# A fused retention and swish-MLP kernel whose every engine issues in an order written out by hand

## The chip, the cores and the metric

The kernel runs on one core of a Trainium2 chip. The metric is the device time of one execution in microseconds (us), as the median of several runs; the profile is of one further execution. The engines are named as the profile names them: PE (matrix multiply; PEld is its weight loads), DVE (vector), ACT (scalar, activations), POOL (GpSimd) and SP (the queue that issues most DMAs).

## What is computed

Eight batches of eight heads, 576 positions, head width 64. Retention without softmax, then a two-layer MLP with a swish whose slope is learned for each hidden unit. The MLP's rows are the 4608 positions, its columns the heads side by side (512).

```python
scores = scale * np.matmul(q, k.transpose(0, 1, 3, 2))
Dmat = np.where(rel >= 0, gamma[:, None, None] ** rel[None, :, :], 0.0)
x = np.matmul(scores * Dmat[None, :, :, :], v)   # then heads side by side: [4608, 512]
h = x @ w_in                                      # 512 -> 2048
g = h * (1.0 / (1.0 + np.exp(-beta * h)))
out = g @ w_out                                   # 2048 -> 512
```

## The kernel before

The decay is split into a factor on q (gq, which also holds the scale) and one on v (gv), so a batch of 576 rows is walked in five chunks: four of 128 rows and a short one of 64. A state carries what earlier chunks add. `attn_chunk(b, c)` does one chunk in these steps:

- prepare (L154 to L160): qn = q times gq, kn = k cast to bf16, vpad = v times gv, spread so that each head pair has its own columns. In batch 0 qn is made on DVE and kn on ACT, later all three on POOL.
- T (L165): eight PE transposes; ACT copies the result out of PSUM (qkT, L169, 1.0 us).
- sc (L177): eight 64-row score matmuls; DVE applies the causal mask (R, L181, twice).
- O (L189, L194): four matmuls with the state (sbd) and eight with vpad; DVE casts the sum into xT (L199), the MLP's input.
- st (L208): four matmuls that add to the state; ACT copies it twice into sbd (L215). The short chunk has none.

The MLP works in nine blocks of 512 rows. `moe_up(m)` has 16 groups of four 512-column matmuls (ph, L229), each followed by a Silu on ACT (gT, L231); `moe_down(m)` has four outputs of 16 matmuls each (po, L239), copied by DVE (ot, L242) and stored through SP (L243). All ph and po tiles share three PSUM buffers; T, O and st have one buffer each, sc two.

The weights come in four 1 MB pieces each, w_in (L126) and w_out (L132), through three staging buffers; DVE casts each w_in piece in one instruction (L127) and scales each w_out piece in four (L135). Chunks are loaded as three DMAs of 256 KB (q, k, v, L60) into seven staging buffers.

The order of each engine's instructions is chosen by the framework's scheduler from priorities that follow the program text: batch 0, then for each later batch its loads, its five chunks, and the up and down of the block before. Only within a chunk's sc, O and st matmuls is PE's order fixed by hand. Loads of w_out stand behind the chunks of batch 1 on SP.

Of the kernel before, what the change touches and what calls it, by code (L numbers as in the profile page):

```python
# [11 lines left out]
F32 = mybir.dt.float32  # L12
# [7 lines left out]
def kernel(  # L20
# [15 lines left out]
    P = 128  # L36
# [26 lines left out]
    for c in range(NC):  # L63
        load_chunk(0, c)
# [3 lines left out]

    ident_f = consts.tile([P, P], F32, name="ident_f")
# [20 lines left out]

    NV = 3
    vpads = []
    for i in range(NV):
        vp = consts.tile([P, H, P], BF16, name=f"vpad{i}")
        nc.gpsimd.memset(vp[:], 0.0)
        vpads.append(vp)

    NS = 2
    sbds = []
    for i in range(NS):  # L100
        s = consts.tile([P, HP, P], BF16, name=f"sbd{i}")
        nc.gpsimd.memset(s[:], 0.0)
        sbds.append(s)
# [19 lines left out]
    w_out_r = moe_w_out.rearrange("(fo fi) n -> fi fo n", fi=P)  # L123
    for g in range(WG):
        t = stage.tile([P, KO, FG], F32, name="wt", tag="wt", bufs=3)
        nc.sync.dma_start(t[:], w_in_r[:, :, g * FG:(g + 1) * FG])  # L126
        nc.vector.tensor_copy(w_in_sb[:, :, g * FG:(g + 1) * FG], t[:])  # L127

    def load_w_out():
        for g in range(WG):  # L130
            t = stage.tile([P, KO, d_model], F32, name="wt", tag="wt", bufs=3)
            nc.sync.dma_start(t[:], w_out_r[:, g * KO:(g + 1) * KO, :])  # L132
            for i in range(KO):
                fo = g * KO + i
                nc.vector.tensor_scalar(w_out_sb[:, fo, :], t[:, i], rbeta_sb[:, fo:fo + 1], None, ALU.mult)  # L135
# [4 lines left out]
    cnt = [0]  # L140

    def attn_chunk(b, c):
        c0, cL = chunks[c]
        t = qkv_tiles.pop((b, c))
        first = b == 0
        qn = sb.tile([P, H, D], BF16, name="qn", tag="qn", bufs=2)
        kn = sb.tile([P, H, D], BF16, name="kn", tag="kn", bufs=3)
        vp = vpads[cnt[0] % NV]
# [4 lines left out]
        eq = nc.vector if first else nc.gpsimd  # L153
        eq.tensor_tensor(qn[:cL], t[:cL, 0], gq_b, ALU.mult)  # L154
# [4 lines left out]
        nc.gpsimd.tensor_tensor(vp4[:cL], t[:cL, 2].rearrange("p (pr two) d -> p pr two d", two=2),  # L159
                                gv_b.rearrange("p (pr two) d -> p pr two d", two=2), ALU.mult)  # L160

        T = psum.tile([P, 2, HP, P], BF16, name="T", tag="T", bufs=1)
        for i, src in enumerate((qn, kn)):
            for p in range(HP):
                nc.tensor.transpose(T[:, i, p, :cL],  # L165
                                    src[:cL, 2 * p:2 * p + 2, :].rearrange("p h d -> p (h d)"),
                                    ident[:cL, :cL])
        qkT = sb.tile([P, 2, HP, P], BF16, name="qkT", tag="qkT", bufs=3)
        nc.scalar.copy(qkT[:, :, :, :cL], T[:, :, :, :cL])  # L169

        R = sb.tile([P, 2, HP, P], BF16, name="R", tag="R", bufs=2)
        sc = [psum.tile([P, HP, P], F32, name="sc", tag="sc", bufs=2) for _ in range(2)]
        with tc.manual_schedule(engines={PE}):
            for p in range(HP):
                for j in range(2):
                    r = slice(j * D, (j + 1) * D)
                    nc.tensor.matmul(sc[j][:cL, p, :cL], qkT[r, 1, p, :cL], qkT[r, 0, p, :cL],  # L177
                                     start=True, stop=True, skip_group_check=True)
# [5 lines left out]
        with tc.manual_schedule(engines={PE}):  # L184
            n = 0
            if c > 0:
                sbd = sbds[(cnt[0] - 1) % NS]
                for p in range(HP):
                    nc.tensor.matmul(O[:, p, :cL], sbd[:, p, :], qkT[:, 0, p, :cL],  # L189
                                     start=(n == 0), stop=False, skip_group_check=True)  # L190
                    n += 1
            for p in range(HP):
                for j in range(2):
                    nc.tensor.matmul(O[:, p, :cL], vp[:cL, 2 * p + j, :], R[:cL, j, p, :cL],  # L194
                                     start=(n == 0), stop=(p == HP - 1 and j == 1),
                                     skip_group_check=True)
                    n += 1
        n0 = b * S + c0
        nc.vector.tensor_copy(xT[:, :, n0:n0 + cL], O[:, :, :cL])  # L199

        if c < NC - 1:
            if c == 0:
                st = psum.tile([P, HP, P], F32, name="st", tag="st", bufs=1)
                state_ps[b] = st
            st = state_ps[b]
            with tc.manual_schedule(engines={PE}):
                for p in range(HP):
                    nc.tensor.matmul(st[:, p, :],  # L208
                                     kn[:cL, 2 * p:2 * p + 2, :].rearrange("p h d -> p (h d)"),
                                     vp4[:cL, p], start=(c == 0 and p == 0), stop=True,  # L210
                                     skip_group_check=True)
            sbd = sbds[cnt[0] % NS]
            for j in range(2):
                r = slice(j * D, (j + 1) * D)
                nc.scalar.copy(sbd[r, :, j * D:(j + 1) * D], st[r, :, j * D:(j + 1) * D])  # L215
        cnt[0] += 1
# [4 lines left out]
    def moe_up(m, fos):  # L221
        m0 = m * MB
# [3 lines left out]
        for fo in fos:  # L226
            ph = psum.tile([P, MB], F32, name="ph", tag="mm", bufs=3)
            for ko in range(KO):
                nc.tensor.matmul(ph[:], w_in_sb[:, ko, fo * P:(fo + 1) * P], xT[:, ko, m0:m0 + MB],  # L229
                                 start=(ko == 0), stop=(ko == KO - 1))  # L230
            nc.scalar.activation(gT[:, fo, :], ph[:], ACT.Silu, scale=beta_sb[:, fo:fo + 1])  # L231

    def moe_down(m):
        m0 = m * MB
        gT = gts.pop(m)
        for ms in range(MB // P):
            po = psum.tile([P, d_model], F32, name="po", tag="mm", bufs=3)
            for fo in range(FO):
                nc.tensor.matmul(po[:], gT[:, fo, ms * P:(ms + 1) * P], w_out_sb[:, fo, :],  # L239
                                 start=(fo == 0), stop=(fo == FO - 1))  # L240
            ot = sb.tile([P, d_model], F32, name="ot", tag="ot", bufs=3)
            nc.vector.tensor_copy(ot[:], po[:])  # L242
            nc.sync.dma_start(out[m0 + ms * P:m0 + (ms + 1) * P, :], ot[:])  # L243

    for c in range(NC):
        attn_chunk(0, c)
    for b in range(1, B + 1):
        if b < B:
            for c in range(NC):
                load_chunk(b, c)  # L250
                if b == 1 and c == NC - 1:
                    load_w_out()
            for c in range(NC):
                attn_chunk(b, c)
        moe_up(b - 1, range(FO))
        moe_down(b - 1)
    for m in range(B, NMB):
        moe_up(m, range(FO))
        moe_down(m)
# [30 lines left out]
```

## Time and profile before

| | us |
|---|---|
| median of 3 runs | 362.81 |
| range of the runs | 362.46 to 363.98 |
| the profiled execution, its time | 362.31 |
| its span, first to last instruction | 360.6 |
| PE busy in the span | 335.3 |
| ACT busy | 160.7 |
| DVE busy | 112.5 |
| POOL busy | 102.6 |

Work on the row of PE includes the time in which a matmul drains while the next already runs, so its busy time is no measure of how densely matmuls follow each other; the distances between starts are. The mean granted TensorE clock over the span is 0.962 of full speed.

### The profile page before, as it was taken

Reading aid. Unit: us, or ns where it says so; the run is one execution under the profiler, and the core shown is the slowest. Engines: PE = TensorE matmul, PEld = TensorE weight load, DVE = VectorE, ACT = ScalarE, POOL = GpSimd, SP = SyncE. Lnnn points to the kernel's source line nnn. Section 1 sums busy time; section 2 is a strip of 40 time slices with the busy share of each in tenths; the row PEclk is TensorE's granted clock in tenths of the full one; section 3 lists DMA queues with packets and bytes.
Section 4 is the critical chain, followed back from the end, with each engine's and each line's share of the span. In section 5 each row is a group of like instructions: output and inputs, shape, how many; then the busy total and the mean of one; then the engine's idle time right before and its main releaser. Section 6 shows DMA issues by size and latency. Waiting matters only on the chain.

```text
span 360.6 us, 5795 instructions
## 1 busy us (share of the span) xinstructions
PE 335.3 (93%) x2369; PEld 175.9 (49%) x2369; DVE 112.5 (31%) x196; ACT 160.7 (45%) x257; POOL 102.6 (28%) x124
## 2 busy tenths in 40 slices
PE   1768967999999999999999999999999999999995
PEld 1643455345544644465446544654466444444442
DVE  4565144724422630164025402450146011011011
ACT  2653843017720864076506660567047703703810
POOL 6211760026832761085007600670051000000000
PEclk9976975799999999999999999999999999999999
DMA  9998995769938995599569951300110011011002
GB/s 175 211 351 209 219 235 208 191 163 219 203 73 200 179 202 92 157 241 192 114 166 206 215 100 58 106 0 2 58 60 2 0 58 60 0 58 59 2 34 82
DMA packets 121978, 46.52 MB, mean 129 GB/s; under 512 B 113232, under 2 KB 113248, under 8 KB 121952
## 3 DMA queue, kind: packets, MB, share of 16 engines
q1 hardware_dynamic: 121920, 46.15, 56.2%
q8 instruction: 18, 0.29, 0.4%
q14 instruction: 8, 0.07, 0.1%
q10 hardware_dynamic: 32, 0.01, 0.0%
HBM read 36.71 MB, written 9.44 MB: 128 GB/s over the span
## 4 chain that ended last, share of the span: by engine, by line
PE 88%; ACT 5%; DVE 3%; DMA 1%; SPq 1%; issue 1%; POOL 0%; ACTq 0%
PE po L239 35%; PE ph L229 34%; PE O L194 6%; PE T L165 5%; PE sc L177 4%; ACT qkT L169 4%; PE O L189 2%; PE st L208 2%; DVE R L181 1%; DMA qkvn<-in_k_dram 1%; SPq L60 1%; ACT gT L231 0%; DVE w_in_sb L127 0%; POOL qn L154 0%; DVE xT L199 0%
## 5 line engine op out<-in xcount | busy, mean ns | idle before, releaser
L229 PE MATMUL ph<-xT,w_in_sb 128*128 128x512 bf16 x576 | 140.2, 384 | 1.7 <-DVE w_in_sb L127 1.7
L231 ACT ACTIVATE gT<-ph,beta_sb 128x512 bf16<-128x512 f32 x144 | 98.9, 687 | 67.4 <-PE ph L229 66.7
L239 PE MATMUL po<-w_out_sb,gT 128*128 128x512 bf16 x576 | 127.5, 383 | 0.9 <-DVE w_out_sb L135 0.9
L239 PEld LDWEIGHTS <-gT 128*128 128x128 bf16 x576 | 56.8, 99 | 69.9 <-issue 3.1
L169 ACT COPY qkT<-T 128x1024 bf16<-128x1024 bf16 (+1 forms) x40 | 36.9, 924 | 100.0 <-PE T L165 100.0
L229 PEld LDWEIGHTS <-w_in_sb 128*128 128x128 bf16 x576 | 53.0, 99 | 56.2 <-issue 3.1
L242 DVE COPY ot<-po 128x512 f32<-128x512 f32 x36 | 24.7, 691 | 168.6 <-PE po L239 168.6
L154 POOL TENSOR_TENSOR qn<-qkvn,gq 128x512 bf16<-128x512 f32 (+1 forms) x35 | 36.6, 1046 | 127.6 <-issue 45.1
L181 DVE TENSOR_TENSOR R<-sc,causal 128x512 bf16<-128x512 f32 (+1 forms) x80 | 47.0, 628 | 35.0 <-PE sc L177 35.0
L159 POOL TENSOR_TENSOR vpad<-qkvn,gv 128x512 bf16<-128x512 f32 (+1 forms) x40 | 41.8, 1045 | 30.4 <-DMA qkvn<-in_v_dram 23.6
L199 DVE CAST xT<-O 128x512 bf16<-128x512 f32 (+1 forms) x40 | 25.5, 638 | 31.9 <-PE O L194 31.8
L194 PE MATMUL O<-R,vpad 128*128 128x128 bf16 (+1 forms) x320 | 31.7, 226 | 2.4 <-DVE R L181 2.2
L194 PEld LDWEIGHTS <-vpad 128*128 128x128 bf16 (+1 forms) x320 | 23.1, 103 | 13.9 <-issue 6.8
L215 ACT CAST sbd<-st 64x256 bf16<-64x256 f32 x64 | 23.4, 366 | 8.8 <-PE st L208 8.0
L177 PE MATMUL sc<-qkT 64*128 64x128 bf16 (+1 forms) x320 | 17.3, 226 | 9.5 <-ACT qkT L169 8.8
L158 POOL CAST kn<-qkvn 128x512 bf16<-128x512 f32 (+1 forms) x35 | 21.3, 607 | 11.0 <-DMA qkvn<-in_k_dram 10.6
L177 PEld LDWEIGHTS <-qkT 64*128 64x128 bf16 (+1 forms) x320 | 10.0, 102 | 20.5 <-ACT qkT L169 18.2
L165 PE MATMUL T<-ident,qn 128*128 128x128 bf16 (+1 forms) x160 | 16.1, 226 | 3.4 <-DVE qn L154 3.3
L165 PE MATMUL T<-ident,kn 128*128 128x128 bf16 (+1 forms) x160 | 17.7, 227 | 0.0
L165 PEld LDWEIGHTS <-qn 128*128 128x128 bf16 (+1 forms) x160 | 10.4, 102 | 9.2 <-DVE qn L154 3.6
L208 PE MATMUL st<-vpad,kn 128*128 128x128 bf16 x128 | 13.6, 230 | 0.0
L189 PE MATMUL O<-qkT,sbd 128*128 128x128 bf16 (+1 forms) x128 | 12.4, 223 | 0.1
(32 smaller groups left out, 59.7 us busy)
## 6 DMA issues: line engine op xcount, KB each, us to landing
out_dram<-ot SPq DMA_DIRECT2D x36, 256.0 KB, 2.0
qkvn<-in_q_dram SPq DMA_DIRECT2D x32, 256.0 KB, 4.9
qkvn<-in_k_dram SPq DMA_DIRECT2D x32, 256.0 KB, 5.1
qkvn<-in_v_dram SPq DMA_DIRECT2D x32, 256.0 KB, 5.1
wt<-in_moe_w_in_dram SPq DMA_DIRECT2D x4, 1024.0 KB, 8.3
wt<-in_moe_w_out_dram SPq DMA_DIRECT2D x4, 1024.0 KB, 7.2
qkvn<-in_q_dram SPq DMA_DIRECT2D x8, 128.0 KB, 4.5
qkvn<-in_k_dram SPq DMA_DIRECT2D x8, 128.0 KB, 4.2
```

What stands on the lines that cost most here:

```text
L154: eq.tensor_tensor(qn[:cL], t[:cL, 0], gq_b, ALU.mult)
L159: nc.gpsimd.tensor_tensor(vp4[:cL], t[:cL, 2].rearrange("p (pr two) d -> p pr two d", two=2), gv_b.rearrange("p (pr two) d -> p pr two d", ...
L165: nc.tensor.transpose(T[:, i, p, :cL], src[:cL, 2 * p:2 * p + 2, :].rearrange("p h d -> p (h d)"), ident[:cL, :cL])
L169: nc.scalar.copy(qkT[:, :, :, :cL], T[:, :, :, :cL])
L177: nc.tensor.matmul(sc[j][:cL, p, :cL], qkT[r, 1, p, :cL], qkT[r, 0, p, :cL], start=True, stop=True, skip_group_check=True)
L181: nc.vector.tensor_tensor(R[:cL, j, :, :cL], sc[j][:cL, :, :cL], m_b, ALU.mult)
L194: nc.tensor.matmul(O[:, p, :cL], vp[:cL, 2 * p + j, :], R[:cL, j, p, :cL], start=(n == 0), stop=(p == HP - 1 and j == 1), skip_group_check ...
L199: nc.vector.tensor_copy(xT[:, :, n0:n0 + cL], O[:, :, :cL])
L229: nc.tensor.matmul(ph[:], w_in_sb[:, ko, fo * P:(fo + 1) * P], xT[:, ko, m0:m0 + MB], start=(ko == 0), stop=(ko == KO - 1))
L231: nc.scalar.activation(gT[:, fo, :], ph[:], ACT.Silu, scale=beta_sb[:, fo:fo + 1])
L239: nc.tensor.matmul(po[:], gT[:, fo, ms * P:(ms + 1) * P], w_out_sb[:, fo, :], start=(fo == 0), stop=(fo == FO - 1))
L242: nc.vector.tensor_copy(ot[:], po[:])
```

## The change

All engines now run under a manual schedule: every instruction stands on its engine in the order in which the program text issues it. The text is rewritten for that.

- `attn_chunk` is split into steps: `pre` (qn, kn, vpad), `a_T`, `a_sc`, `a_st`, `a_O`. The MLP is split into groups: `up(m, fo)` with four matmuls, `down(m, ms, f0)` with four. `merged` walks a list of groups and puts the attention steps between them at given group numbers: `attn_steps` puts `pre` four groups ahead of a_T, a_sc two groups behind a_T, and a_st and a_O two groups behind a_sc.
- Only chunks 0 to 3 run ahead of the MLP, with `pre` two chunks ahead and 22 extra 512-column matmuls on a zero tile in all (`warm_up`): 12 at the start and 2 at five places. Then the 16 up groups of block 0 follow, with chunks 4 and 5 between the last of them.
- Block 1's up is done in two parts: its first 192 columns (chunks 4 and 5) before block 0's down, its other 320 after it. Chunks 6, 7 and 8 stand between these.
- From block 2 on, the chunks that block m+1 needs (4 or 5) are spread evenly over block m's 32 groups.
- SP loads four chunks, w_in, three chunks, w_out, and then one chunk for each that has been prepared. The staging buffers of weights grow from three to four and also hold the outputs (`ot`, four to a tile). Of each weight piece three quarters are cast on DVE and one on POOL.
- Three small things: gq's scale moves into the exponent as a bias; the second half of O walks one half of R after the other; two memsets move to DVE.

SP, the loads of w_out; each qkvn tile is a chunk, each wt tile a piece of 1 MB. Before:

```order
L60 DMA qkvn_450<-in_q_dram 64x8x64
L60 DMA qkvn_450<-in_k_dram 64x8x64
L60 DMA qkvn_450<-in_v_dram 64x8x64
L132 DMA wt_454<-in_moe_w_out_dram 128x4x512
L132 DMA wt_460<-in_moe_w_out_dram 128x4x512
L132 DMA wt_466<-in_moe_w_out_dram 128x4x512
L132 DMA wt_472<-in_moe_w_out_dram 128x4x512
```

The changed kernel:

```order
L63 DMA qkvn_152<-in_q_dram 128x8x64
L63 DMA qkvn_152<-in_k_dram 128x8x64
L63 DMA qkvn_152<-in_v_dram 128x8x64
L133 DMA wt_435<-in_moe_w_out_dram 128x4x512
L133 DMA wt_437<-in_moe_w_out_dram 128x4x512
L133 DMA wt_467<-in_moe_w_out_dram 128x4x512
L133 DMA wt_469<-in_moe_w_out_dram 128x4x512
```

Before, w_out stands behind ten chunks (qkvn_450 is the short one of batch 1); now behind seven (qkvn_152 is chunk 6).

DVE at the end of the first chunks, where the MLP begins. Before:

```order
L199 CAST xT<-O 128x4x128
L181 TENSOR_TENSOR R<-sc,causal 64x4x64 x2
L199 CAST xT<-O 128x4x64
L127 CAST w_in_sb<-wt 128x4x512 x4
L181 TENSOR_TENSOR R<-sc,causal 128x512 x2
```

The changed kernel:

```order
L221 TENSOR_TENSOR R<-sc,causal 128x512 x2
L129 CAST w_in_sb<-wt 128x512 x3
L242 CAST xT<-O 128x4x128
L129 CAST w_in_sb<-wt 128x512 x9
L221 TENSOR_TENSOR R<-sc,causal 64x4x64 x2
```

The first weights are now cast between R and xT of chunk 3, where before all five chunks went first; the short chunk's R follows the weights.

ACT in the middle of the kernel: Silu (gT), copies of T (qkT) and of the state (sbd). Before, a batch from its third full chunk on:

```order
L169 COPY qkT<-T 128x1024
L215 CAST sbd_129<-st 64x4x64 x2
L231 ACTIVATE gT<-ph,beta_sb 128x512
L169 COPY qkT<-T 128x1024
L215 CAST sbd_127<-st 64x4x64 x2
L231 ACTIVATE gT<-ph,beta_sb 128x512
L169 COPY qkT<-T 128x8x64
L231 ACTIVATE gT<-ph,beta_sb 128x512 x13
```

The changed kernel, block 2's up:

```order
L275 ACTIVATE gT<-ph,beta_sb 128x512 x4
L261 CAST sbd_126<-st 64x4x64 x2
L275 ACTIVATE gT<-ph,beta_sb 128x512 x3
L205 COPY qkT<-T 128x8x64
L275 ACTIVATE gT<-ph,beta_sb 128x512 x6
L205 COPY qkT<-T 128x1024
L275 ACTIVATE gT<-ph,beta_sb 128x512 x3
```

Before, a batch's copies stand close together with a Silu between two chunks and then 13 Silus in a row; now three to six Silus stand between one copy and the next.

The diff, cut; the steps a_T, a_sc, a_st and a_O hold the instructions of `attn_chunk`, unchanged but for the order inside O.

```diff
+    ctx.enter_context(tc.manual_schedule())
...
+    NQ = 7
+    order = [(b, c) for b in range(B) for c in range(NC)]
+    for b, c in order[:4]:
+        load_chunk(b, c)
...
+    nc.scalar.activation(gq[:], lg[:], ACT.Exp, bias=lscale[:])
...
+    def cast_w_in(g):
+        t = wts.pop(g)
+        for ko in range(KO):
+            e = nc.gpsimd if ko == KO - 1 else nc.vector
+            e.tensor_copy(w_in_sb[:, ko, g * FG:(g + 1) * FG], t[:, ko])
...
+    for b, c in order[4:NQ]:
+        load_chunk(b, c)
+
+    def warm_up(n):
+        ph = psum.tile([P, MB], F32, name="ph", tag="mm", bufs=3)
+        for _ in range(n):
+            nc.tensor.matmul(ph[:], warm[:, :P], warm[:], start=True, stop=True, skip_group_check=True)
...
+        for j in range(2):
+            for p in range(HP):
+                nc.tensor.matmul(O[:, p, :cL], vp[:cL, 2 * p + j, :], R[:cL, j, p, :cL],
+                                 start=(n == 0), stop=(j == 1), skip_group_check=True)
...
+    def up(m, fo, t0=0, tn=MB):
...
+    def down(m, ms, f0, fn=4):
...
+            if ms == 0:
+                ots[m] = stage.tile([P, MB // P, d_model], F32, name="ot", tag="wt", bufs=4)
...
+    def merged(fill, *streams):
+
+        todo = sorted((x for st in streams for x in st), key=lambda x: x[0])
+        for n, f in enumerate(fill):
+            while todo and todo[0][0] <= n:
+                todo.pop(0)[1]()
+            f()
+        for _, step in todo:
+            step()
...
+    def attn_steps(i, at, gap=2.0):
+
+        return [(at - 4, F(pre, i)), (at - 3.9, F(load_next, i)), (at, F(a_T, i)), (at + gap, F(a_sc, i)),
+                (at + 2 * gap, F(a_st, i)), (at + 2 * gap, F(a_O, i))]
+
+    warm_up(12)
+    betas()
+    pre(0)
+    a_T(0)
+    nc.gpsimd.memset(vpads[2][:], 0.0)
+    pre(1)
+    for i in range(4):
+        warm_up(2)
+        a_sc(i)
+        a_st(i)
+        if i < 3:
+            a_T(i + 1)
+            if i < 2:
+                pre(i + 2)
+        else:
+            cast_w_in(0)
+            warm_up(2)
+        a_O(i)
+
+    fill = [F(up, 0, fo) for fo in range(FO)]
+    merged(fill, [(2, F(cast_w_in, 1)), (5, F(cast_w_in, 2)), (9, F(cast_w_in, 3))],
+           [(5.1 + g / 10, F(load_w_out, g)) for g in range(2)],
+           [(9.1 + g / 10, F(load_w_out, g)) for g in range(2, WG)],
+           [(9.5, F(pre, 4)), (12, F(a_T, 4)), (14, F(a_sc, 4)), (16, F(a_O, 4))],
+           [(9.6, F(pre, 5)), (15, F(a_T, 5)), (16.1, F(a_sc, 5))], [(9.7, F(pre, 6))])
+    for i in range(5):
+        load_next(i)
+
+    q1 = S + chunks[0][1] - MB
+    a_st(5)
+    a_O(5)
...
+    fill = [F(up, 1, fo, 0, q1) for fo in range(FO)]
+    fill += [F(down, 0, ms, f0) for f0 in range(0, FO, 4) for ms in range(3)]
+    fill += [F(down, 0, 3, f0) for f0 in range(0, FO, 4)]
+    n1 = len(fill)
+    fill += [F(up, 1, fo, q1, MB - q1) for fo in range(FO)]
+    fill += [F(down, 1, ms, f0) for ms in range(MB // P) for f0 in range(0, FO, 4)]
+    streams = [[(4, F(cast_w_out, 0)), (10, F(cast_w_out, 1)), (18, F(cast_w_out, 2)), (21, F(cast_w_out, 3))],
+               [(0, F(a_T, 6)), (4, F(a_sc, 6)), (8, F(a_st, 6)), (8, F(a_O, 6))],
+               attn_steps(7, 23), attn_steps(8, 27)]
...
+    for m in range(2, NMB):
+        base = len(fill)
+        fill += [F(up, m, fo) for fo in range(FO)]
+        fill += [F(down, m, ms, f0) for ms in range(MB // P) for f0 in range(0, FO, 4)]
+        if m + 1 < NMB:
+            todo = list(range(done, need(m + 1)))
+            streams += [attn_steps(i, base + n * 31 / len(todo)) for n, i in enumerate(todo)]
+            done = need(m + 1)
+    merged(fill, *streams)
```

## Rows read from the trace of the kernel before

**Rows 1.** Chain that ended last, in order of time: start us, us, what.

```profile
63.66 15.68 PE po L239 x64
...
79.33 0.45 PE T L165 x8
...
139.73 13.81 PE po L239 x64
...
153.54 0.46 PE T L165 x8
...
190.53 0.46 PE T L165 x8
...
342.96 13.83 PE po L239 x64
...
356.81 0.69 DVE ot L242
```

**Rows 2.** Stretches: busy us of each engine, granted TensorE clock, DMA share, GB/s.

```profile
23.00:33.00 10.00, 7.38 (x46) 3.58 (x45) 5.70 (x8) 3.71 (x5) 0.00 (x0) 0.50 0.77 272
...
51.00:66.00 15.00, 10.86 (x94) 7.38 (x93) 8.61 (x18) 4.07 (x7) 1.86 (x3) 0.50 0.56 198
```

**Rows 3.** Timeline of the first 30 us: start us, us, engine, line, what, waits.

```profile
17.61 1.04 POOL L159 TENSOR_TENSOR vpad<-qkvn,gv 128x512 bf16<-128x512 f32 x1 [2.74 <-DMA qkvn<-in_v_dram]
...
17.75 0.76 ACT L215 CAST sbd<-st 64x256 bf16<-64x256 f32 x2 [0.88 <-PE st L208]
...
21.46 1.29 DVE L181 TENSOR_TENSOR R<-sc,causal 128x512 bf16<-128x512 f32 x2 [1.48 <-PE sc L177]
...
23.75 0.69 DVE L199 CAST xT<-O 128x512 bf16<-128x512 f32 x1 [0.40 <-PE O L194]
...
27.08 3.60 DVE L127 CAST w_in_sb<-wt 128x2048 bf16<-128x2048 f32 x3
...
28.36 1.89 PE L229 MATMUL ph<-xT,w_in_sb 128*128 128x512 bf16 x4 [1.65 <-DVE w_in_sb L127]
```

**Rows 4.** Stretches of 1 us, loading chunks, then weights (columns as above).

```profile
12.00:13.00 1.00, 1.00 (x11) 0.79 (x10) 1.00 (x2) 0.94 (x3) 0.00 (x0) 1.00 1.38 217
...
24.00:25.00 1.00, 0.33 (x9) 0.17 (x8) 0.44 (x1) 0.70 (x2) 0.00 (x0) 0.50 1.05 387
```

**Rows 5.** Timeline where batch 4 meets the first half of block 3.

```profile
153.38 0.39 PE L165 MATMUL T<-ident,qn 128*128 128x128 bf16 x4
...
153.82 0.39 PE L208 MATMUL st<-vpad,kn 128*128 128x128 bf16 x4
...
154.05 1.03 PE L229 MATMUL ph<-xT,w_in_sb 128*128 128x512 bf16 x4
...
154.08 1.01 ACT L169 COPY qkT<-T 128x1024 bf16<-128x1024 bf16 x1 [13.63 <-PE T L165]
...
155.15 0.40 PE L177 MATMUL sc<-qkT 64*128 64x128 bf16 x8
...
155.48 0.40 PE L165 MATMUL T<-ident,qn 128*128 128x128 bf16 x4
```

**Rows 6.** The same chain: pieces of a full and a short chunk.

```profile
122.72 0.39 PE O L194 x7
...
126.07 0.23 PE T L165 x8
...
128.69 0.24 PE sc L177 x7
...
129.68 0.12 PE O L189 x4
...
130.68 0.31 PE O L194 x7
```

**Rows 7.** Costliest groups of the page: two kinds of work on ACT.

```profile
L231 ACT ACTIVATE gT<-ph,beta_sb 128x512 bf16<-128x512 f32 x144 | 98.9, 687 | 67.4 <-PE ph L229 66.7
...
L215 ACT CAST sbd<-st 64x256 bf16<-64x256 f32 x64 | 23.4, 366 | 8.8 <-PE st L208 8.0
```

More of the change, by code (lines that the diff above doesn't have):

```diff
@@ L123 @@
     w_out_r = moe_w_out.rearrange("(fo fi) n -> fi fo n", fi=P)
-    for g in range(WG):
[L125 to L135, printed above, removed]
+    wts = {}
@@ L152, in attn_chunk @@
         gv_b = gv[:cL, c, :].unsqueeze(2).to_broadcast([cL, H, D])
[L153 to L154 removed]
+        (nc.vector if first else nc.gpsimd).tensor_tensor(qn[:cL], t[:cL, 0], gq_b, ALU.mult)
         if first:
@@ L169, in attn_chunk, with a_sc @@
         nc.scalar.copy(qkT[:, :, :, :cL], T[:, :, :, :cL])
+        L["qT"], L["kT"] = qkT[:, 0], qkT[:, 1]
+    def a_sc(i):
+        b, c = order[i]
+        c0, cL = chunks[c]
+        L = live[i]
         R = sb.tile([P, 2, HP, P], BF16, name="R", tag="R", bufs=2)
         sc = [psum.tile([P, HP, P], F32, name="sc", tag="sc", bufs=2) for _ in range(2)]
[L173 to L178, printed above, removed]
+        for p in range(HP):
+            for j in range(2):
+                r = slice(j * D, (j + 1) * D)
+                nc.tensor.matmul(sc[j][:cL, p, :cL], L["kT"][r, p, :cL], L["qT"][r, p, :cL],
+                                 start=True, stop=True, skip_group_check=True)
         m_b = causal[:cL, :cL].unsqueeze(1).to_broadcast([cL, HP, cL])
@@ L181, in attn_chunk @@
             nc.vector.tensor_tensor(R[:cL, j, :, :cL], sc[j][:cL, :, :cL], m_b, ALU.mult)
-        O = psum.tile([P, HP, P], F32, name="O", tag="O", bufs=1)
[L184 to L191, printed above, removed]
-            for p in range(HP):
[L193 to L197, printed above, removed]
+        L["R"] = R
@@ L198, in attn_chunk @@
         n0 = b * S + c0
         nc.vector.tensor_copy(xT[:, :, n0:n0 + cL], O[:, :, :cL])
[L201 to L215, printed above, removed]
@@ L216, in attn_chunk, with a_st @@
-        cnt[0] += 1
+        del live[i]
+    def a_st(i):
+        b, c = order[i]
+        c0, cL = chunks[c]
+        L = live[i]
+        if c == NC - 1:
+            return
+        if c == 0:
+            state_ps[b] = psum.tile([P, HP, P], F32, name="st", tag="st", bufs=1)
+        st = state_ps[b]
+        for p in range(HP):
+            nc.tensor.matmul(st[:, p, :], L["kn"][:cL, 2 * p:2 * p + 2, :].rearrange("p h d -> p (h d)"),
+                             L["vp4"][:cL, p], start=(c == 0 and p == 0), stop=True,
+                             skip_group_check=True)
+        sbd = sbds[i % NS]
+        for j in range(2):
+            r = slice(j * D, (j + 1) * D)
+            nc.scalar.copy(sbd[r, :, j * D:(j + 1) * D], st[r, :, j * D:(j + 1) * D])
@@ L225, in moe_up @@
         gT = gts[m]
[L226 to L259, printed above, removed]
+        x0 = m * MB + t0
+        ph = psum.tile([P, MB], F32, name="ph", tag="mm", bufs=3)
@@ new lines @@
+    done = 9
+    need = lambda m: min(len(order), next((i + 1 for i, (b, c) in enumerate(order)
+                                          if b * S + chunks[c][0] + chunks[c][1] >= (m + 1) * MB), len(order)))
+    todo = list(range(done, need(2)))
+    streams += [attn_steps(i, n1 + n * 30 / len(todo)) for n, i in enumerate(todo)]
+    done = need(2)
+    for m in range(2, NMB):
[6 more added lines that the diff above has]
+            done = need(m + 1)
```

133 lines of the change are left out of this document (93 added, 40 removed).

## The prediction

> **What bounds the kernel now.** I read the chain of work in order of time first: it lies on PE nearly throughout, so the question is how much of PE's time is work that has to be done. In the chain 64 matmuls of 512 columns take 13.81 us when nothing disturbs them, 0.863 us for a group of four [rows 1]. The MLP is 18 such halves, 18 x 13.81 = 248.6 us. An attention chunk is priced from starts in a dense stretch [rows 5]: eight T from 153.38 to 153.82, 0.44; four st to 154.05, 0.23; eight sc from 155.15 to 155.48, 0.33; eight O with vpad at 0.39 for seven, 0.45 [rows 6]; four O with the state as half the T, 0.22. That is 1.67 for a full chunk, 1.45 for the first of a batch (no state to read). The short one is 0.23 + 8/7 x 0.24 + 0.12 + 8/7 x 0.31 = 0.98 [rows 6]. A batch is 1.45 + 3 x 1.67 + 0.98 = 7.44, eight are 59.5. So 308 us of the 360.6 are dense PE work.
>
> Where the other 52 lie shows in the chain [rows 1]. Block 0's down begins at 63.66, with 13.81 + 2 x 7.44 = 28.7 of work done: 35.0 lost. From there to the end of the last po, 342.96 + 13.83 = 356.79, there are 293.1 us for 17 x 13.81 + 6 x 7.44 = 279.4: 13.7 lost. A batch in the middle, from 153.54 to 190.53, takes 36.99 for 27.62 + 7.44, so 1.9 are lost in each. One such loss can be seen: T begins at 153.38, ACT copies it from 154.08 for 1.01, sc begins at 155.15, and four ph fill only part of the gap [rows 5]. The last 3.8 us are copy and store of the last output. [...]
>
> **The start.** Before, all of batch 0 comes ahead of the first ph at 28.36, and all of batch 1 ahead of the first po. Now only four chunks come first. Their twelve DMAs are the first twelve on SP in both kernels, so the last v lands at 17.61 as before, where POOL waited for it [rows 3], and its k one DMA (262 KB at 217 GB/s [rows 4] = 1.2 us) earlier, at 16.4. From there the chain on hand-ordered engines is: kn cast 0.7 (taken as long as xT's), four T 0.22, the two sbd copies queued on ACT 0.76, qkT 1.01, sc 0.33, R 1.29, three w_in casts on DVE of a quarter of 1.2 each, 0.9, and xT 0.69 [rows 3, 5]; with about nine hand-overs of 0.06 (154.08 + 1.01 to 155.15 [rows 5]) that is 6.4, or 22.8. The first MB of w_in follows chunk 3 at 387 GB/s [rows 4], 2.7 us, and is there at 20.3, in time. A half clock doubles sc and T in this gappy stretch, so I take **23.5** for the first ph (22.5 to 26). The 22 warm-up matmuls cost 22 x 0.22 to 0.43 of PE time, but stand where PE waits for landings, qkT or R; uncovered, the last two pairs would cost 1.7, which is in the 26.
>
> The first ph will run at half clock, I think: the warm-ups are too few to make these chunks dense. Before, the first down after such a stretch took 15.68 instead of 13.81 [rows 1], and the first four ph 1.89 with their drain [rows 3]. I take **2.0** lost, from 0 to 2.3.
>
> **Weights and chunks in time.** From 20.3 three more MB of w_in land by 28.4, chunks 4 to 6 (2.5 x 786 KB at 217) by 37.5, w_out by 48.3. Up groups 4, 8 and 12 want the later pieces at 27, 30.5 and 34 or after; chunk 4's T stands at group 12, some 10 us behind the first ph, and its loads are done at 30.2. The first down comes at about 51.5, its last quarter of w_out is wanted nine groups later. Chunk 7 lands at 51.9 and is wanted at 57.5. POOL, with 2.7 us of preparation for a chunk and a fourth of each cast, sits on none of these. Stores and loads share SP, so a load queues behind a store that waits for ot, but each load is seven chunks ahead of its use. All of this I cost at nothing; if SP came later than I think by 5 us, PE would wait those 5.
>
> **Where PE must wait in the hand order.** (a) Between chunks 4 to 6: T of chunk 5 has one up group and O of chunk 4 (0.86 + 0.4) before its sc, but ACT has a Silu and then the copy to do; then O of chunk 5 has only st in front, while R takes 1.29. Walking ACT, DVE and PE with these durations I get 0.3 + 1.1 = 1.4. (b) In the first part of block 1's up a group of 192 columns takes PE about 0.33 and its Silu about 0.4 (estimate between the 0.366 of a 256-column copy and the 0.687 of a 512-column Silu [rows 7]); with qkT and sbd on ACT in the same 16 groups PE ends 1.4 late. (c) The 320-column part: 0.3. Together **3.1**.
>
> (d) The steady part. T is followed by two groups, so sc comes 0.44 + 2 x 0.863 = 2.17 after T's start. With an idle ACT it could come 1.77 after it [rows 5]. If the Silu of the group before is still running, ACT is free 0.94 instead of 0.70 after T's start, which makes 2.01: still 0.16 to spare. O comes 1.73 + 0.45 behind sc, R needs 1.29. So most of the 1.9 per batch goes away; I leave 0.05 per chunk, **1.5** (0 to 9.5, see the first rival).
>
> **The sum.** 23.5 + 248.6 + seven batches and a short chunk, 7 x 7.44 + 0.98 = 53.1, + 2.0 + 3.1 + 1.5 = 331.8 for the end of the last po; + 3.8 = 335.6 of span; the profiled execution took 362.31 for a span of 360.6, so + 1.7 = 337.3; the median is 0.5 above it: **337.8**. The gain of 25.0 is some 14 at the start (at 63.66 the changed kernel has done 28.7 + 14 of work) and 11 in the steady part.
>
> [...]
>
> **Rivals.** First: ACT runs one Silu late in the up groups. Then sc waits 0.69 - 0.16 = 0.53 at each of the 18 or so chunks whose T stands there: 9.5 more, **347** (342 to 352). For it: 16 Silus are 11.0 us and 2.6 chunks of copies 4.6, 15.6 of the 18 us of an up phase. Against it: three PSUM buffers let PE run ahead, and downs have no Silu. Chance 0.17.
>
> Second: the MLP starts late. The clock is at half through the first chunks, every step between landing and landing is longer, first ph at 26.5: **341**, and 345 with w_out pushed back as well. For it: the clock of before [rows 2]. Chance 0.10.
>
> Third, slower: ACT becomes the bound. Its strict order lets a Silu that waits for PE hold the copy that PE waits for; with two Silus and not one ahead, each of 36 chunks pays 2 x 0.69 - 0.16 = 1.2, 43 in all: **381**. It is slower than before from 0.7 per chunk on. Against it: PE's order puts the group's matmuls ahead of each such Silu. Chance 0.05.
>
> [...] Chance 0.01.
>
> Fifth: no half clock at the first ph, no waits but (a): **331**. Chance 0.04.
>
> **How the numbers follow.** Forecast 0.61 (332 to 342), first rival 0.17, second 0.10, slower 0.06, faster than 332 0.04, and 0.02 that waits eat just the gain. The range goes from 331 to 347: it leaves out the slower cases, the equal one and the upper half of the first rival, about 0.17. About 0.5% is what a measurement here can tell from no change. Faster 0.92, same 0.02, slower 0.06.
>
> **What would show it.** First ph near 23.5; first po near 51 instead of 63.66; no half clock after about 28; between two down halves of the middle blocks 27.6 plus 6 to 8 us instead of 37; sc's wait for qkT nearly gone from the waits. Wrong would be: a chain with qkT or R in every chunk, DVE or POOL waiting for w_out or chunk 7, or a second stretch at half clock.

## The result and the profile after

The changed kernel takes 338.43 us (median of 4 runs, 338.11 to 338.8); the kernel before, run beside it, 362.63. The ratio is 0.934, with a 95% interval of 0.929 to 0.939. The profiled execution took 338.8 for a span of 337.1, at a mean granted clock of 0.994.

The chain in order of time (start us, us, what) answers [rows 1]: the way to the first po, the first po of block 1, the T at the ends of two blocks in the middle, the last po. A T that stands at the same place in two blocks bounds one whole block.

```profile
35.56 7.35 DMA wt<-in_moe_w_out_dram
...
46.28 2.66 PE ph L273 x32
48.94 6.04 PE po L285 x28
...
78.69 0.86 PE po L285 x4
...
131.47 0.45 PE T L201 x8
...
165.55 0.45 PE T L201 x8
...
201.41 0.45 PE T L201 x8
...
319.47 13.83 PE po L285 x64
```

Block 0's down begins at 48.94 and not at 63.66. By then PE has done 13.81 of up, 10.56 of chunks (batch 0 and chunks 5 and 6) and 5.18 of block 1's up (192 of 512 columns), 29.55 in all, so 19.4 are lost up to there, where 35.0 were lost before: 15.6 gained. The last po ends at 319.47 + 13.83 = 333.30. From 48.94 that is 284.36 for 278.55 of dense work (17 x 13.81 - 5.18 of MLP, and 48.96 for 26 full and 7 short chunks), so 5.8 are lost where 13.7 were: 7.9 gained. Together that is the 23.5 by which the last po ends earlier.

The stretches (busy us of PE, PEld, DVE, ACT and POOL with counts, granted clock, DMA share, GB/s) answer [rows 2]:

```profile
8.00:12.00 4.00, 3.36 (x29) 2.26 (x30) 1.75 (x4) 1.87 (x3) 1.72 (x2) 0.57 1.37 218
23.00:33.00 10.00, 9.82 (x47) 4.25 (x46) 4.53 (x9) 7.72 (x12) 3.97 (x5) 1.00 1.06 256
...
51.00:66.00 15.00, 14.97 (x118) 8.08 (x117) 6.80 (x12) 3.49 (x6) 11.72 (x14) 1.00 1.24 204
```

Both stretches that were at 0.50 are at 1.00. PE is busy for 14.97 of the 15 us from 51 to 66, where it was for 10.86. The half clock is left only among the first chunks, 0.57 from 8 to 12.

The timeline of the start answers [rows 3]:

```profile
22.28 9.01 PE L273 MATMUL ph<-xT,w_in_sb 128*128 128x512 bf16 x41 [1.34 <-DVE xT L242]
```

The first ph comes at 22.28 (28.36 before) behind xT, and 41 of them follow in 9.01 us, 0.22 each, at a granted clock of 1.00 from 22 to 24 and from 23 to 33. Before, the first four took 1.89, their drain included [rows 3].

The waits (who, for whom: us of idle time, times, us of the longest) show where the steady gain is:

```profile
PE sc L217 <- ACT qkT L205: 0.4, 2, 0.2
```

The same two waits of the kernel before:

```profile
PE sc L177 <- ACT qkT L169: 8.8, 8, 2.4
```

sc hardly waits for ACT's copy any more (0.4 for 8.8, and the 0.4 lies in the first 30 us). And a chunk in the middle of the changed kernel, which answers [rows 5]:

```profile
156.70 0.39 PE L201 MATMUL T<-ident,qn 128*128 128x128 bf16 x4
...
157.15 1.89 PE L285 MATMUL po<-w_out_sb,gT 128*128 128x512 bf16 x8
...
157.35 1.01 ACT L205 COPY qkT<-T 128x1024 bf16<-128x1024 bf16 x1 [3.54 <-PE T L201]
...
158.97 0.23 PEld L217 LDWEIGHTS <-qkT 64*128 64x128 bf16 x8 [0.42 <-issue]
158.97 0.40 PE L217 MATMUL sc<-qkT 64*128 64x128 bf16 x8
159.30 1.90 PE L285 MATMUL po<-w_out_sb,gT 128*128 128x512 bf16 x8
...
161.04 0.39 PE L255 MATMUL st<-vpad,kn 128*128 128x128 bf16 x4
```

The copy ends at 158.36, while the two groups of po still run (157.15 + 8 x 0.2158 = 158.88). sc begins 2.27 us behind T's start. From 159.30 to st at 161.04 there are 8 x 0.2158 and nothing else. The one gap left is that of 0.09 to 0.10 between the last po and sc; it comes back below.

### The profile page after: what moved, and what is told of

It reads as the page before. It is cut to its first block, busy times and chain, and to the rows that moved or that the text cites. A ratio compares the mean times of both kernels' runs of the same rounds, so it can differ in the third digit from the quotient of the medians.

```text
span 337.1 us, 6009 instructions
## 1 busy us (share of the span) xinstructions
PE 325.6 (97%) x2455; PEld 174.0 (52%) x2455; DVE 114.0 (34%) x202; ACT 163.1 (48%) x272; POOL 115.0 (34%) x132
## 4 chain that ended last, share of the span: by engine, by line
PE 84%; DMA 7%; SPq 4%; issue 1%; DVE 1%; ACT 1%; POOL 0%; POOLq 0%
PE po L285 38%; PE ph L273 32%; DMA qkvn<-in_q_dram 4%; PE O L238 4%; PE T L201 4%; SPq L63 4%; PE sc L217 3%; DMA wt<-in_moe_w_out_dram 2%; PE st L255 2%; PE O L233 2%; SPq L122 1%; ACT gT L275 1%; DVE w_out_sb L141 0%; DVE R L221 0%; ACT qkT L205 0%
## 5 line engine op out<-in xcount | busy, mean ns | idle before, releaser
L273 PE MATMUL ph<-xT,w_in_sb 128*128 128x512 bf16 (+2 forms) x640 | 134.2, 358 | 1.7 <-DVE xT L242 1.7
L285 PE MATMUL po<-w_out_sb,gT 128*128 128x512 bf16 x576 | 133.6, 380 | 0.0
L275 ACT ACTIVATE gT<-ph,beta_sb 128x512 bf16<-128x512 f32 (+2 forms) x160 | 102.0, 645 | 41.2 <-PE ph L273 39.9
L273 PEld LDWEIGHTS <-w_in_sb 128*128 128x128 bf16 x640 | 58.4, 98 | 55.5 <-issue 1.6
L285 PEld LDWEIGHTS <-gT 128*128 128x128 bf16 x576 | 53.3, 98 | 57.9
L238 PE MATMUL O<-R,vpad 128*128 128x128 bf16 (+1 forms) x320 | 23.7, 214 | 1.4 <-DVE R L221 1.2
L238 PEld LDWEIGHTS <-vpad 128*128 128x128 bf16 (+1 forms) x320 | 18.2, 97 | 2.8 <-issue 2.2
L217 PE MATMUL sc<-qkT 64*128 64x128 bf16 (+1 forms) x320 | 15.5, 217 | 0.6 <-ACT qkT L205 0.4
L201 PE MATMUL T<-ident,kn 128*128 128x128 bf16 (+1 forms) x160 | 14.9, 216 | 0.3 <-POOL kn L185 0.3
L255 PEld LDWEIGHTS <-kn 128*128 128x128 bf16 x128 | 9.5, 99 | 6.6 <-issue 0.2
```

The source lines that it names most:

```text
L201: nc.tensor.transpose(T[:, j, p, :cL], src[:cL, 2 * p:2 * p + 2, :].rearrange("p h d -> p (h d)"), ident[:cL, :cL])
L217: nc.tensor.matmul(sc[j][:cL, p, :cL], L["kT"][r, p, :cL], L["qT"][r, p, :cL], start=True, stop=True, skip_group_check=True)
L255: nc.tensor.matmul(st[:, p, :], L["kn"][:cL, 2 * p:2 * p + 2, :].rearrange("p h d -> p (h d)"), L["vp4"][:cL, p], start=(c == 0 and p == 0 ...
L273: nc.tensor.matmul(ph[:, :tn], w_in_sb[:, ko, fo * P:(fo + 1) * P], xT[:, ko, x0:x0 + tn], start=(ko == 0), stop=(ko == KO - 1))
L275: nc.scalar.activation(gT[:, fo, t0:t0 + tn], ph[:, :tn], ACT.Silu, scale=beta_sb[:, fo:fo + 1])
```

## The experiments

The edits are against the changed kernel ("after", 338.43). The kernel before took 362.6 to 363.1 beside each of them.

**The warm-ups.** The 22 extra matmuls are taken out.

```diff
-    warm_up(12)
...
-        warm_up(2)
...
-            warm_up(2)
```

> The changed kernel without its 22 extra matmuls on the zero tile (they feed nothing). Theory: they are what kept the granted clock at full through the first chunks, where my prediction had taken 2.0 us for a first up at half clock and the trace showed none. Without them the clock is at half from some point of the first 20 us, the first ph groups take 1.7 us and not 0.86 for some us, and the first steps are longer too: 340.5 to 343. Rival: the four chunks alone are dense enough, or the clock comes up with the first ph at no cost: 338 to 339.

Measured: 339.65 (339.04 to 340.34), ratio to the kernel before 0.937 (0.934 to 0.940). By the medians it is some 1.2 slower, which lies between the two expectations; but the runs below that keep the time of after, with all warm-ups, spread from 337.67 to 340.38 (and one of 341.95), so the size is uncertain. Four of its stretches (columns as above):

```profile
8.00:12.00 4.00, 3.46 (x36) 2.53 (x33) 2.37 (x5) 2.27 (x4) 1.62 (x2) 1.00 1.37 218
...
20.00:22.00 2.00, 0.51 (x7) 0.31 (x5) 2.00 (x5) 1.43 (x2) 0.61 (x1) 1.00 1.05 388
22.00:24.00 2.00, 1.79 (x7) 0.71 (x7) 0.16 (x1) 0.63 (x1) 0.00 (x0) 0.75 1.04 388
24.00:26.00 2.00, 2.00 (x6) 0.74 (x5) 1.51 (x3) 0.75 (x2) 0.87 (x1) 0.50 1.05 386
```

And its chain up to the first po:

```profile
22.21 12.22 PE ph L273 x48
...
49.59 2.59 PE po L285 x12
```

Here the half clock does fall on the first ph, after 20 to 22, in which PE was busy for 0.51 of 2 us. From 8 to 12, on the other hand, the clock is at 1.00, where after, with the warm-ups, has 0.57. So in these two executions the warm-ups did not keep the half clock away: it lay among the first chunks instead of on the first ph. Three other runs, all with the warm-ups, have it in either place: the execution of 341.95 in both (0.50 from 10 to 15, 0.55 from 26 to 28), the late w_out among the first chunks (0.83 from 10 to 20, 1.00 from 20 to 30), the two changes together on the first ph (0.79 from 22 to 30).

The 48 ph take 12.22 instead of 10.4 (48 x 0.2158), but the first po is only 0.65 later than in after. Of the 1.8, 0.9 are taken up where PE waits for chunk 4 in after (the ph behind that T starts at 33.76 there and at 34.69 here), and 0.3 where it waits for R of chunk 6.

**The spacing of the steps.** One group instead of two between T, sc and O, and three instead of two:

```diff
-    def attn_steps(i, at, gap=2.0):
+    def attn_steps(i, at, gap=1.0):
```

> One change: one MLP group instead of two between T and sc, and between sc and O. Theory: two groups (2.17 us from T's start to sc) just cover T, hand-over and the copy qkT (1.77 with ACT idle, 2.01 behind a Silu). With one group sc is due 1.30 after T's start and waits 0.47 to 0.71, and O is due 1.3 after sc with R needing 1.3 and hand-overs: 0.6 to 0.9 for each of 33 chunks, 20 to 30 us: 358 to 368, all the gain or nearly. Rival: the even spread is what helps and PE runs on with little wait: under 345.

Measured: 350.93 (350.04 to 351.85), ratio 0.968 (0.965 to 0.971): 12.5 slower, 0.38 for each of 33 chunks. The direction was right, the size half. A chunk of it, from its timeline:

```profile
153.25 0.39 PE L201 MATMUL T<-ident,qn 128*128 128x128 bf16 x4
...
155.10 0.40 PE L217 MATMUL sc<-qkT 64*128 64x128 bf16 x8 [0.37 <-ACT qkT L205]
...
156.53 0.73 PE L238 MATMUL O<-R,vpad 128*128 128x128 bf16 x8
```

sc comes 1.85 behind T, where T and one group fill 0.45 + 0.86 = 1.31. Most falls on sc: 0.54, of which 0.10 is the gap that is there in any case. O, behind one group and st, loses 0.12 (0.73 for 0.61). That is 0.56 for this chunk, more than the mean of 0.38. Over the whole run PE's sc waits 8.9 us for qkT (0.4 in after), and O 2.2 us for R (1.2 in after).

> One change: three groups instead of two between T and sc and between sc and O, from chunk 9 on. Theory: two groups already cover the copies (0.16 us to spare), so a third brings nothing: 337.5 to 339.5. Rival: the 4 us that the steady part takes beyond my sum are waits of sc for the copy, 0.1 a chunk; then three groups give them back: 334 to 336.

Measured: 338.53 (338.42 to 341.95), ratio 0.936 (0.931 to 0.941): no difference from after. Two groups already cover copy and mask, so what is lost in the steady part is not a wait for them. Its profiled execution was the one of 341.95; the other three took 338.42 to 338.63. Its stretches:

```profile
10.00:15.00 5.00, 4.75 (x39) 3.30 (x37) 2.39 (x5) 3.38 (x6) 2.22 (x2) 0.50 1.37 217
...
24.00:26.00 2.00, 0.73 (x4) 0.37 (x4) 2.00 (x6) 0.36 (x1) 0.01 (x1) 1.00 1.05 387
26.00:28.00 2.00, 2.00 (x7) 0.72 (x6) 1.54 (x4) 0.69 (x1) 0.87 (x1) 0.55 1.14 327
```

And its chain:

```profile
25.27 12.21 PE ph L273 x48
...
52.40 6.04 PE po L285 x28
```

Up to the first po this kernel's order is that of after. In this execution the half clock held from 10 to 15, among the first chunks, and the first ph came at 25.27 instead of 22.28. From 24 to 26 PE was busy for 0.73 of 2 us, and the ph ran at half clock again (0.55 from 26 to 28, 12.21 us for 48). The first po is 3.5 later than in after: 3.0 from the late first ph and 0.5 from the clock behind it. So the same order of work can meet the clock in two ways, and the 22 warm-ups do not rule the worse one out. The chains of six other runs that go like after as far as the first ph have it between 22.44 and 24.74.

**An even spread or a packed one.** From block 2 on, a chunk begins every third group, and the rest of the block runs without any:

```diff
-            streams += [attn_steps(i, base + n * 31 / len(todo)) for n, i in enumerate(todo)]
+            streams += [attn_steps(i, base + n * 3) for n, i in enumerate(todo)]
```

> One change, from block 2 on: the chunks of a block follow each other every three groups from its first group on, where they were spread evenly every 6 to 8; the two groups inside a chunk stay. Theory: what PE needs are the two groups between dependent steps; ACT then has 3 Silus and 1.8 us of copies in 3 x 0.863 + 1.8 us, just enough: 338 to 340. Rival: the even spread itself gave the steady part of the gain, since ACT, DVE or POOL (2.7 us of preparation in 4.4) fall behind when chunks crowd: over 343.

Measured: 338.99 (338.18 to 340.36), ratio 0.935 (0.932 to 0.939): no difference. Whether chunks begin three groups apart or six to eight makes no difference here, as long as the two groups inside a chunk stay.

**st between the groups and sc.** st moves from behind sc to right ahead of it, to see what makes the 0.10 gap:

```diff
-... (at, F(a_T, i)), (at + gap, F(a_sc, i)),
-                (at + 2 * gap, F(a_st, i)), (at + 2 * gap, F(a_O, i))]
+... (at, F(a_T, i)), (at + gap, F(a_st, i)), (at + gap, F(a_sc, i)),
+                (at + 2 * gap, F(a_O, i))]
```

> One change: st of a chunk stands right ahead of its sc instead of ahead of O. The trace shows 0.10 us in front of nearly every sc in which PE does nothing and the first weight load of sc (64 rows) is late. Theory: that load doesn't run ahead of a 128-row matmul, whatever stands there, so the gap stays: 338.0 to 338.9 and 0.10 between st and sc. Rival: the gap comes from the long 512-column matmul ahead of it; then it goes, 0.1 for 33 chunks: 335 to 335.5.

Measured: 338.81 (338.27 to 340.38), ratio 0.936 (0.932 to 0.939). The same, and the gap stays:

```profile
158.13 0.43 PEld L255 LDWEIGHTS <-kn 128*128 128x128 bf16 x4
158.35 0.39 PE L255 MATMUL st<-vpad,kn 128*128 128x128 bf16 x4
158.66 0.23 PEld L217 LDWEIGHTS <-qkT 64*128 64x128 bf16 x8
158.67 0.40 PE L217 MATMUL sc<-qkT 64*128 64x128 bf16 x8
```

The weight load of st (128 rows) begins 0.22 ahead of its first matmul, under the po before it. That of sc (64 rows) begins together with its matmul, 0.09 after st has run out (158.35 + 4 x 0.055 = 158.57). The copy had ended at 157.83 (156.82 + 1.01), so the gap is neither a wait for ACT nor a matter of the long matmuls in front.

**The output weights.** w_out is loaded behind ten chunks, as before the change, instead of seven:

```diff
-           [(5.1 + g / 10, F(load_w_out, g)) for g in range(2)],
-           [(9.1 + g / 10, F(load_w_out, g)) for g in range(2, WG)],
...
+        if i == 2:
+            for g in range(WG):
+                load_w_out(g)
```

> One change: the four loads of w_out stand behind chunks 7, 8 and 9 on SP, that is behind ten chunks as in the kernel before. Each piece then lands 2.5 chunks at 3.6 us = 9 us later. Theory: what decides is DVE's fixed order, where the cast of the first piece stands ahead of R of chunk 6; R, O and the rest of the up part wait for it, and the first po comes 8 to 9 us later than at 48.9: 346 to 348. Rival: only the first po and its later quarters wait, with the last one due 7.8 us after the first: 4 to 5 us, 342.5 to 343.5. Second rival: loads were not tight and little changes: under 340.

Measured: 348.92 (348.59 to 351.83), ratio 0.965 (0.959 to 0.970): 10.5 slower, a little more than the theory said. The chain:

```profile
44.88 7.05 DMA wt<-in_moe_w_out_dram
...
52.35 1.31 DVE w_out_sb L141 x2
53.66 0.61 DVE R L221
...
55.50 3.97 PE ph L273 x32
59.47 6.04 PE po L285 x28
```

It isn't po that waits first: the cast of w_out stands on DVE ahead of chunk 6's R, so O of chunk 6 and the up groups behind it wait for the DMA as well. After the pause these 32 ph run at the lower clock (3.97 us; 2.66 in after), and the granted clock from 50 to 60 is 0.60. In after the chain to the first po takes the same way, through the first piece of w_out, with the DMA done at 42.91 instead of 51.93.

To separate the two, the first cast is moved behind chunk 6's O, in after alone and then together with the late load:

```diff
-    streams = [[(4, F(cast_w_out, 0)), (10, F(cast_w_out, 1)), ...
+    streams = [[(8.1, F(cast_w_out, 0)), (10, F(cast_w_out, 1)), ...
```

> One change: the cast of the first w_out piece stands behind chunk 6's O on the engines, no longer ahead of its R. Theory: in the trace R of chunk 6 begins 1.2 us after its sc is done because DVE casts first; without that the first po comes 0.6 to 1.1 us sooner: 337.2 to 337.9. Rival: the Silus of the 192-column groups on ACT end last there anyway, and nothing changes: 338.2 to 338.7.

Measured: 338.57 (337.67 to 339.28), ratio 0.934 (0.931 to 0.937). The profiled execution has the first po at 47.94, 1.0 sooner than after, and took 337.67; over all runs no gain can be told.

> Two changes together: the late w_out loads of the earlier run (348.9) and the cast of the first piece behind chunk 6's O. Theory: of the 10.5 us that the late loads cost, the part that comes through DVE's order (R of chunk 6 behind the cast, and the half clock after that wait) goes, and only the first po and its later quarters wait for weights: 342.5 to 345. Rival: the loads are late by themselves and the place of the cast does not matter: 348 to 349.

Measured: 346.12 (345.06 to 346.37), ratio 0.954 (0.951 to 0.957), between the two expectations. Late weights alone cost 346.12 - 338.57 = 7.6, the place of their cast on DVE another 2.8. Some 1.3 of the 2.8 are the half clock behind that wait (3.97 - 2.66 for the 32 ph); here the clock is at 1.00 from 46 to 62. Now po itself waits for the cast, 2.41 at the first and 0.44 and 0.26 at later ones:

```profile
52.67 1.71 DVE L141 TENSOR_SCALAR w_out_sb<-wt,rbeta_sb 128x512 bf16<-128x512 f32 x3 [3.80 <-DMA wt<-in_moe_w_out_dram]
...
53.22 0.39 PE L285 MATMUL po<-w_out_sb,gT 128*128 128x512 bf16 x1 [2.41 <-DVE w_out_sb L141]
```

**MLP groups between the chunks of batch 1.** Chunks 6 to 8 run in a row, without MLP groups between their steps, ahead of block 0's down; block 1's up is then one part, and the casts of w_out stand behind chunk 8:

```diff
-    fill = [F(up, 1, fo, 0, q1) for fo in range(FO)]
-    fill += [F(down, 0, ms, f0) for f0 in range(0, FO, 4) for ms in range(3)]
+    for i in (6, 7, 8):
+        ...
+        a_T(i)
+        a_sc(i)
+        a_st(i)
+        a_O(i)
+    fill = [F(down, 0, ms, f0) for f0 in range(0, FO, 4) for ms in range(3)]
...
-    fill += [F(up, 1, fo, q1, MB - q1) for fo in range(FO)]
+    fill += [F(up, 1, fo) for fo in range(FO)]
...
-    streams = [[(4, F(cast_w_out, 0)), (10, F(cast_w_out, 1)), ...
+    streams = [[(0, F(cast_w_out, 0)), (1, F(cast_w_out, 1)), ...
```

> One change: chunks 6, 7 and 8 run one after the other ahead of block 0's down, as batch 1 did before the change, and block 1's up is one part behind that down; weights are loaded early as in the changed kernel. Theory: most of the gain at the start is that MLP groups stand between these chunks, which come in slowly (chunk 8 is loaded at about 57). The first po moves from 48.9 to about 62.5, with 5 us of up work not yet done by then and 3.6 of chunks 7 and 8 done: 15 us lost, 351 to 355. Rival: the early w_out is what counts, and with it the chunks' order matters little: under 345.

Measured: 358.53 (357.72 to 358.76), ratio 0.989 (0.986 to 0.992): 20.1 slower, more than the theory said, with the rest of the change untouched. Its chain:

```profile
38.28 13.62 DMA qkvn<-in_q_dram
...
54.41 1.02 ACT qkT L205
```

Its first po, from its timeline:

```profile
64.12 0.58 PE L285 MATMUL po<-w_out_sb,gT 128*128 128x512 bf16 x1 [1.54 <-DVE w_out_sb L141]
```

And its stretch that answers [rows 2]:

```profile
50.00:67.00 17.00, 9.58 (x69) 6.38 (x71) 7.66 (x11) 3.49 (x6) 13.18 (x12) 0.50 1.13 205
```

PE waits for chunk 7 until its T can run at 53, then copy and mask of chunks 7 and 8 lie bare, at a clock of 0.50, and the first po comes at 64.12: the picture of the kernel before (63.66, and 0.50 from 51 to 66). Two things make this case worse than a bare order: the wait for chunk 7 is longer than it need be, since w_out is now loaded ahead of it, and the first cast of w_out stands on DVE behind chunk 8's xT, so that po waits 1.54 for it. The same order with w_out behind chunk 8 was not tried, so how the 20.1 divide between load, cast and bare steps is open.

**An attempt at a better version.** T of chunk 4 one group later (it waits for its loads), the cast of w_out later, the last output in two halves so that its copy and store start sooner:

```diff
-           [(9.5, F(pre, 4)), (12, F(a_T, 4)), (14, F(a_sc, 4)), (16, F(a_O, 4))],
+           [(9.5, F(pre, 4)), (13, F(a_T, 4)), (14.9, F(a_sc, 4)), (16, F(a_O, 4))],
...
+        fill += [F(down_last, m, MB // P - 1)] * last
```

> Three small edits to the changed kernel, each for a wait that its trace shows: T of chunk 4 one up group later (it waits 0.7 for POOL, which waits for the chunk's loads), the first w_out cast behind chunk 6's O (first po 1.0 sooner in the profile of that run), and the last output in two halves of 256 columns, so that the last copy and store are half as long (3.8 us lie behind the last po, 0.3 to 0.6 of it goes). If the waits are worth what they last: 336 to 337. Rival: what is freed is waited for at the next late load (chunk 5 or w_out): 337.5 to 338.5.

Measured: 338.22 (337.71 to 339.84), ratio 0.933 (0.931 to 0.936). Not to be told from after. In the profiled execution the shorter last output does what was expected of it (3.1 us behind the last po instead of 3.8), but that is no more than the executions differ among themselves. The first po comes at 48.67, 0.3 sooner than in after; PE waits ahead of it for R of chunk 5 (39.27 to 40.56) and for its xT (41.02 to 41.72), one behind the other.

## Why the prediction was right, point by point

The forecast was 337.8; 338.43 was measured. That is closer than its terms were, and in part luck. The first po came 2.5 sooner than forecast and the part behind it lost 4.0 more, so the last po ends 1.5 late. Of these 1.5, 0.9 go by luck again: I had put the median 0.5 above the profiled execution, and it lies 0.4 below it.

| | predicted | measured in the trace |
|---|---|---|
| first ph | 23.5 | 22.28 |
| lost from there to the first po | 2.0 + 1.4 + 1.4 = 4.8 | 26.66 - 23.1 = 3.6 |
| first po | about 51.5 | 48.94 |
| lost from there to the last po | 0.3 + 1.5 = 1.8 | 5.8 |
| end of the last po | 331.8 | 333.30 |
| last copy and store | 3.8 | 3.8 |
| gain at the start, in the steady part | 14, 11 | 15.6, 7.9 |

**The mechanism.** What gave the gain was as predicted: MLP groups stand between steps that before stood bare. For the steady part the run with one group instead of two shows it: 12.5 come back with nothing else changed. For the start it is the run without groups between batch 1's chunks, 20.1, which holds the late chunk 7 and the late cast as well; and the late w_out, 10.5, shows that the order of the loads has its share. These overlap and do not add up to the gain. That only four chunks run ahead of the first ph, which comes 6.1 sooner, was not undone in a run of its own, nor were the casts on POOL and the three small things.

**The half clock at the first ph, 2.0: mis-sized.** It did not come in the profiled execution of after. Where it came, without warm-ups and in the execution of 341.95, it was worth 0.65 and 0.5 at the first po, which fits that PE waits behind it for chunk 4 in any case. What I put into it lies a step earlier: a start that meets the clock badly moves the first ph, by 3.0 there, within the 22.5 to 26 that I had allowed (22.28 lies just below). All the warm-ups together are worth about 1.2 by the medians, within the spread of the executions.

**The waits (a) and (b), 2.8: (a) came, (b) did not.** From the trace's starts, R and then xT of chunk 5 cost 1.5, where (a) was 1.4. ACT being late in the 192-column part, my (b), does not show. Instead R of chunk 6 stands behind the first cast of w_out on DVE:

```profile
42.93 1.71 DVE L141 TENSOR_SCALAR w_out_sb<-wt,rbeta_sb 128x512 bf16<-128x512 f32 x3 [1.47 <-DMA wt<-in_moe_w_out_dram]
...
44.57 1.27 DVE L221 TENSOR_TENSOR R<-sc,causal 128x512 bf16<-128x512 f32 x2
```

The four O of its second half start at 45.90, 0.38 after the first four could be through; with a shorter wait ahead of the first half, it costs 0.5. I had costed w_out at nothing because its last quarter is wanted late, and did not ask what stands behind its first cast on DVE. "DVE or POOL waiting for w_out" was one of the signs of being wrong that I had named, and it came: DVE waits 3.6 us for it in three waits, POOL 4.5. The late load shows the price of that place when the DMA is late too: 2.8.

**Weights and chunks "at nothing": nearly.** Chunk 4 was to be loaded by 30.2. POOL still waits for its q before 31.64, and its T begins at 32.99 and 33.54:

```profile
31.64 1.29 POOL L181 TENSOR_TENSOR qn<-qkvn,gq 64x512 bf16<-64x512 f32 x1 [0.22 <-DMA qkvn<-in_q_dram]
```

That is 0.7; moving that T a group later, together with two other edits, gave nothing back that could be told.

**The steady part, 0.05 a chunk: the term that failed.** The distances were right: sc was forecast 2.17 behind T and comes 2.27 behind it. The difference is a price, not a wait. I had costed sc at 0.33 from start to start of dense rows and never looked at how it begins. Behind a 128-row matmul it begins 0.09 to 0.10 late. For 26 full chunks that is 2.6. In a short chunk T, sc and the vpad half of O have 64-row weights, and each of them begins late:

```profile
136.53 3.62 PE L273 MATMUL ph<-xT,w_in_sb 128*128 128x512 bf16 x16
140.08 0.29 PE L201 MATMUL T<-ident,qn 64*128 64x64 bf16 x4
140.21 0.28 PE L201 MATMUL T<-ident,kn 64*128 64x64 bf16 x4
140.42 1.90 PE L273 MATMUL ph<-xT,w_in_sb 128*128 128x512 bf16 x8
142.25 0.31 PE L217 MATMUL sc<-qkT 64*64 64x64 bf16 x8
```

The ph in front end at 136.53 + 16 x 0.2158 = 139.98 and T begins at 140.08; the next eight end at 142.15 and sc begins at 142.25. The vpad half of O begins 0.21 behind the half with the state, which I had priced at 0.12. Behind T there is a gap too: its first four take 0.13, the other four with the step to ph 0.21.

What a short chunk costs in all follows from two blocks. From 131.47 to 165.55 are 34.08; less 27.62 of MLP, two full chunks of 1.77 and the first of a batch, 1.45 + 0.10, the short one is left with 1.37. From 165.55 to 201.41 are 35.86, with one full chunk more: 1.38. I had priced it at 0.98, so 0.39 x 7 = 2.7 more. Together that is 5.3 of the 5.8, where I had allowed 1.5. About 0.4 more is lost from 48.94 to 78.69, where the 320-column part lies; (c) was 0.3.

So what is left in the steady part is nearly all the price of beginning groups with 64-row weights, and that three groups of distance or an early st give nothing back fits it. The kernel before pays it as well:

```profile
128.13 0.55 PE L194 MATMUL O<-R,vpad 128*128 128x128 bf16 x7
...
128.62 0.31 PE L177 MATMUL sc<-qkT 64*64 64x64 bf16 x7
```

Seven O from 128.13 have run out at 128.13 + 7 x 0.055 = 128.52; sc begins 0.10 later, though its copy was done at 127.28, 1.3 us before. Of the 1.9 that each batch lost there, I had taken most for waits that would go; 35.86 - 27.62 - 7.44 = 0.8 of it stay, and the steady gain is 7.9 instead of 11.

**The rivals.** A late ACT in the up groups (347) and ACT as the bound (381) did not come: sc's own wait for qkT is 0.4 in all. With one group instead of two between the steps, a wait for the copy does come, 8.9 us in all. The late MLP start (341) is nearly what the 341.95 of the spacing experiment's execution was. Short matmuls kept the pace at which I had priced them: eight T take the 0.45 from 156.70 to 157.15, 0.056 each, and 0.44 in the kernel before. What the fifth rival (331) asked for nearly came: no half clock at the first ph, and of the waits (a) and little else. The time did not, since the 64-row price was missing from its sum too.

## What to carry to other kernels

Count the PE work that can stand between a step and the one that needs its copy; here two groups of 0.86 us cover a hand-over of 1.8 us, a third gives nothing, one costs 0.38 per chunk. Where loads come slowly, put the dense work between them and not behind them: PE is then busy while they land, and in the profiled execution of the changed kernel its clock was at 1.00 there (from 51 to 66; 0.50 before). On hand-ordered engines look behind each cast that waits for a DMA: what stands next in that queue waits as well, and the price grows as the DMA comes later (0.5 here; 2.8 with the weights late, 1.3 of it through the clock). And price a short piece of work from the end of what stands in front of it to the start of what stands behind it, not by its own starts: the 0.10 ahead of each sc is in the trace of the kernel before, but not in a price taken from dense rows.

## What the runs showed of the hardware

- In the rows shown above, a group of matmuls with 64-row weights behind one with 128-row weights begins 0.09 to 0.10 us late, whether the ones in front are long (po, ph) or short (st); its load begins only with it (158.97 for 158.97 in after, 158.66 for 158.67 with st first). The first 128-row load of st begins 0.22 ahead of its matmul, under the po before it (158.13 for 158.35). Behind the 64-row T of a short chunk the 128-row ph begins some 0.08 late as well (0.21 for four T and the step, 0.13 for four T). Why the 64-row loads begin no sooner in this place is not shown.
- The granted clock at the start differs between executions of the same order of work: 1.00 from 22 to 24 in after, whose first ph comes at 22.28, and 0.55 from 26 to 28 in the execution of 341.95, whose first ph comes at 25.27. The first po lies 3.5 us apart in them (48.94 and 52.40).
- 22 matmuls on a zero tile did not take the half clock away in the profiled executions; it lay in different places with and without them: 0.57 from 8 to 12 with them and 1.00 on the first ph, 1.00 from 8 to 12 without them and 0.50 on the ph from 24 to 26.
